# Sums of phi_k^T [v | 1] in blocks of three heads, or head by head in quarters of the array

## The chip, the cores and the metric

The kernel runs on one core of one Trainium2 chip. The metric is the device time of one execution in microseconds, as the median of several runs. Beside the runs there is one profiled execution, whose trace gives the start and length of each instruction on each engine: TensorE (PE, with its weight loads apart as PEld), VectorE (DVE), ScalarE (ACT), GpSimd (POOL), and the DMA queue that SyncE (SP) issues.

## The reference

Two layers, each an attention step and a dense step, on x of 2048 rows and 640 columns. The attention has 32 heads of 20 columns. Per head, q and k go through a small matrix w_phi and two softmaxes, so that phi has 40 columns:

```python
phi_k = concatenate([softmax(pk), softmax(-pk)], axis=-1)
kv  = einsum("bhsf,bhsd->bhfd", phi_k, v)      # per head: 40 x 20
z   = einsum("bhsf->bhf", phi_k)               # per head: 40
num = einsum("bhqf,bhfd->bhqd", phi_q, kv)
den = einsum("bhqf,bhf->bhq", phi_q, z)[..., None] + 1e-6
o = num / den                                  # then @ wo, and added to x
```

The dense step is x + mish(norm(x) @ w1 + b1) @ w2 with 1536 hidden columns. What matters here is kv and z: for each head, phi_k^T times [v | 1], a sum over all 2048 rows whose result is 40 x 21.

## The kernel before, in words

The rows are worked in 16 tiles of 128 (NT), two to a block (BT), eight blocks (NB). A layer has three parts. attend_first goes over the blocks and makes, for each tile, keys, values and queries: project multiplies the normalized rows with the weights (L344; weights and rows are split into a high and a low fp32r part, so each product is three matmuls), features makes the two softmaxes on ACT, DVE and POOL (L355 to L380), and the last of these steps, on POOL, is the multiplication with the reciprocal sums (L379). Queries are then turned and stored to DRAM (L425 to L429). attend_second reads them back (load, L521), multiplies them with the finished sums (average, L573), divides, and multiplies with wo. dense follows (L695 and L737).

The sum over rows that the change is about stands at the end of keys (L412 to L419). v is a row tile of 32 x 21 columns, each head's 20 values and a one; e is a row tile of 32 x 40 columns of phi_k. For each tile i the loop takes three heads at a time (11 groups g, the last of two heads): the stationary operand is v's 63 or 64 columns of the group, the moving operand is e's 120 columns. Even groups write output partitions 0 to 63, odd ones 64 to 127. What comes out is for three heads at once, 63 x 120, of which only the three blocks of 21 x 40 on the diagonal are wanted. The sums stay in two PSUM banks for the whole of attend_first: kva has pairs 0 to 3 of groups, kvz pairs 4 and 5. The operands are plain fp32.

finish_kv (L532) is the bridge between the two halves of the attention. It is a generator that attend_second advances: DVE copies the two banks to SBUF and multiplies them with a mask that keeps the diagonal blocks (L537); PE transposes the six pieces (L545); ACT and DVE bring them to kvb (L547 to L550), which has the group's 120 rows of phi on its partitions and, per group, 64 columns of head and value. In average, kvb is the moving operand, 63 columns at a time, against 64 rows of turned queries (L573).

The order of the instructions is set by a scheduler with a time model over the whole block (L816). In attend_second and in the first steps the order on PE and SP is that of the program (manual_schedule, L448 and L611). There, finish_kv's steps alternate with those of rest (L503), the projection of the last tile's queries, whose L344 products stand between the sum, the transposes and the first average.

PSUM has eight banks: mm_tile takes two at a time (two buffers, L66), one_tile one (four buffers, L69); kva and kvz are two of those four while the sum runs.

Of the kernel before, what the change touches and what calls it, by code (L numbers as in the profile page):

```python
# [29 lines left out]
HC = D // 2  # L30
EW = 2 * D
GW = 3 * (DH + 1)
GP = 6
VW = H * (DH + 1)
SKEW = 2
LAYERS = 2
# [6 lines left out]
def kernel(  # L43
# [45 lines left out]
    nc.vector.memset(neg_half, -0.5)  # L89
    two = const.tile([P, 1], F32, name="two")  # L90
    nc.vector.memset(two, 2.0)
    mask = const.tile([P, 120], F32, name="mask")

    kvb = const.tile([120, GP, P], F32, name="kvb")

    stats = const.tile([P, NB, 2, BT], F32, name="stats")

# [289 lines left out]
    def attend_first(layer, x_src, first):  # L387


        def fetch_normed(b):  # L390
            if layer:
                return load_turned(n2_d[b], [row_tile] * 3)
            xt = fetch(x_src, b)
            norm_scale(b, [norm_stats(t, xt) for t in range(BT)])
            return xt

        pending = []

        def advance():
            for g in pending[::-1]:  # L400
                try:
                    next(g)
                except StopIteration:
                    pending.remove(g)

        def keys(xts, i, v):
            e = big_tile()
            yield from features(project(xts, i % BT, kv_ws, 0), e, False)
            yield
            if i % BT == 0 and BT < i < NT - BT:  # L410
                yield
            for g in range(G):  # L412
                p, n = divmod(g, 2)
                w, m = (120, 64) if g < 10 else (80, 42)
                acc, c = (kva, 120 * p) if p < 4 else (kvz, 120 * (p - 4))
                nc.tensor.matmul(acc[64 * n:64 * n + m, c:c + w], v[:, GW * g:GW * g + m],  # L416
                                 e[:, 120 * g:120 * g + w],
                                 start=(i == 0 and p in (0, 4)), stop=(i == NT - 1),
                                 skip_group_check=True)  # L419

        def queries(xts, i, ps=None):
            e = query_tile(i)
            yield from features(project(xts, i % BT, q_ws, 0) if ps is None else ps, e, True)

            nc.vector.transpose(e, e)  # L425
            b, t = divmod(i, BT)
            dst = e_d[b].rearrange("(j f) (t q s) -> t q f j s", f=32, t=BT, s=32)
            for q in range(4):
                nc.sync.dma_start(dst[t, q], e[32 * q:32 * q + 32].rearrange("f (j s) -> f j s", s=32))  # L429
                if b == NB - 1:  # L430
                    yield

        def values(xts, i, v):
            vv = v.rearrange("p (h d) -> p h d", d=DH + 1)
            act(vv[:, :, DH], ident[:, :H], AF.Copy, scale=0.0, bias=1.0)
            if i < BT:
                pv = project(xts, i, kv_ws, D, [one_tile(), one_tile()])
                for c in range(2):
                    act(vv[:, c * H // 2:(c + 1) * H // 2, :DH],
                        pv[c][:, :HC].rearrange("p (h d) -> p h d", d=DH), AF.Copy)  # L440
            else:
                pv = project(xts, i % BT, kv_ws, D)
                act(vv[:, :, :DH].rearrange("p (c h) d -> p c h d", c=2),
                    both(pv).rearrange("p c (h d) -> p c h d", d=DH), AF.Copy)
            yield

        if first is None:
            with tc.manual_schedule(engines={mybir.EngineType.SP}):  # L448
                bd = big_tile()[:120, :720].rearrange("p (t c) -> p t c", t=6)
                nc.sync.dma_start(bd[:, :3], phi_bd[:, :3])  # L450
                raw = load_raw(0, range(3))
                xt = fetch_normed(0)
                nc.sync.dma_start(bd[:, 3:], phi_bd[:, 3:])
                raw += load_raw(0, range(3, 6))
                nxt = normed(0, xt).all()
                q_ws = [r2_pair(k) for k in range(KD)]
                fold_phi(q_ws, bd, raw)
                kv_ws = load_v_weights()
                raw = load_raw(1)
            nc.sync.dma_start(mask, head_mask)  # L460
        else:
            nxt, kv_ws = first
            q_ws = load_q_weights()
        for b in range(NB):
            xts = nxt
            order = ("k0", "k1", "v0", "v1", "q0", "q1")
            if b == 0:
                order = ("v0", "q0", "v1", "k0", "q1", "k1")
            elif b == 1:
                order = ("k0", "q0", "k1", "v0", "q1", "v1")  # L470
            elif b == NB - 1:
                order = ("k0", "k1", "v0", "v1", "q0")
            vs = [v_tile() for _ in range(BT)]
            for n, (kind, t) in enumerate(order):
                t = int(t)
                i = b * BT + t
                if b == 0 and n == 1:
                    if layer:
                        load_k_weights(kv_ws)
                if b == 0 and n == 3:  # L480
                    if layer == 0:
                        fold_phi(kv_ws, bd, raw)
                    kva, kvz = one_tile(), one_tile()
                if b == NB - 1 and n == 3:
                    loaded = {0: load(0)}
                if b + 1 < NB:
                    if n == 0:
                        xt = fetch_normed(b + 1)
                    elif n == 2:
                        nxt = xt if layer else normed(b + 1, xt)  # L490
                    elif n > 2:
                        nxt.step()
                g = {"k": lambda: keys(xts, i, vs[t]), "q": lambda: queries(xts, i),
                     "v": lambda: values(xts, i, vs[t])}[kind]()
                next(g)
                advance()
                pending.append(g)
            if b == 1:
                if layer == 0:
                    spill_qk_weights(kv_ws, q_ws)  # L500
                o_ws = load_o_weights()

        def rest():  # L503

            ps = [one_tile(), one_tile()]
            project_half(ps[0], xts, 1, q_ws, 0, 0)
            advance()
            advance()
            yield
            project_half(ps[1], xts, 1, q_ws, 0, 1, range(3))  # L510
            yield
            project_half(ps[1], xts, 1, q_ws, 0, 1, range(3, KD))
            pending.append(queries(xts, NT - 1, ps))
            next(pending[-1])
            while pending:
                yield
                advance()

        return kva, kvz, o_ws, loaded, rest()

    def load(b):  # L521

# [6 lines left out]
        nc.sync.dma_start(tc_[:80, 0], e_d[b][1200:])  # L529
        return [(ta, tb)[g // 5][:, (g % 5) * BLK:(g % 5 + 1) * BLK] for g in range(10)] + [tc_[:, 0]]  # L530

    def finish_kv(kva, kvz, mask):  # L532

        acc, acz = row_tile(), row_tile()
        for src, dst, p1, n, w in ((kva, acc, P, 4, 120), (kvz, acz, P, 1, 120), (kvz, acz, 42, 1, 80)):
            c = 120 if w == 80 else 0
            nc.vector.tensor_tensor(dst[:p1, c:c + n * w].rearrange("p (n w) -> p n w", n=n),  # L537
                                    src[:p1, c:c + n * w].rearrange("p (n w) -> p n w", n=n),
                                    mask[:p1, :w].unsqueeze(1).to_broadcast([p1, n, w]), op=ALU.mult)
        yield  # L540
        for src, q0, n in ((acc, 0, 4), (acz, 4, 2)):
            ps = one_tile().rearrange("p (n c) -> p n c", n=4)
            for q in range(n):
                p1, w = (P, 120) if q0 + q < 5 else (42, 80)
                nc.tensor.transpose(ps[:w, q, :p1], src[:p1, 120 * q:120 * q + w], ident[:p1, :p1])  # L545
            if n == 4:
                act(kvb[:, :4], ps[:120], AF.Copy)  # L547
            else:
                nc.vector.tensor_copy(kvb[:, 4], ps[:120, 0])
                nc.vector.tensor_copy(kvb[:80, 5, :42], ps[:80, 1, :42])  # L550
        yield

    def attend_second(x_src, x_dst, acc, fetches, makes, fetch_next, begin_next):
        kva, kvz, o_ws, loaded, rest = acc
        rows = {}
        div = [None]

# [5 lines left out]
        def average(b, t):  # L563
# [3 lines left out]
            for g in range(G):  # L567
# [3 lines left out]
                for q in range(2):  # L571
                    s0 = t * P + 64 * q
                    nc.tensor.matmul(  # L573
                        po[64 * q:64 * q + 64, c, GW * j:GW * j + w], phs[g][:n, s0:s0 + 64],
                        kvb[:n, g // 2, 64 * (g % 2):64 * (g % 2) + w], start=True, stop=True)
            o = row_tile()
            den = work.tile([P, H], F32, tag="r", name="den", bufs=2)
            pv = [po[:, c, :(DH + 1) * n].rearrange("p (h d) -> p h d", d=DH + 1)
# [30 lines left out]
                return mv  # L609

        with tc.manual_schedule(engines={mybir.EngineType.PE, mybir.EngineType.SP}):  # L611
            kv = finish_kv(kva, kvz, mask)
            next(rest)
            next(kv)
            loaded[1] = load(1)
# [283 lines left out]
```

## Time and profile before

| what | value |
|---|---|
| runs | 1396.43, 1398.02, 1398.83 us; median 1398.02 |
| the profiled execution's own time | 1396.09 us |
| its span, first to last instruction | 1394.3 us |
| mean granted TensorE clock | 0.999 |
| matmuls at L416 as the trace counts them | 704 multiplies, 704 weight loads |

The page gives the busy time of each engine and what it waited for. A group such as "L416 PE MATMUL one<-big,v" is line 416 of the kernel, its engine and operation, the tile it writes (one) and those that it reads (big is e, v is v), and the shape. The ends of matmuls are modelled in the trace, so how fast PE works is read from the starts of successive rows: a row of the timeline has its start, its length up to the end of the last of its instructions, and how many follow each other (x22).

### The profile page before, as it was taken

To read this page: it belongs to the slowest core of one execution; us is meant where nothing else is said; L and a number is where in the kernel's file an instruction comes from. 1 tells how busy PE (TensorE), PEld (TensorE's weight loads), DVE (VectorE), ACT (ScalarE), POOL (GpSimd) and SP (SyncE) were. 2 spreads that over 40 slices of the span, in tenths; PEclk is the share of its full clock that TensorE was granted. 3 is DMA by queue.
4 is the path that set the end of the run, shared out by engine and by line. 5 is a ranking of instruction groups with operands and counts; after the bars stand their busy time and mean duration, and the time that the engine had idled before them with its cause. 6 is when DMAs were issued, how large, how long until landed. Compare 5 with 4: busy or idle time off the path is not lost. (4 is left out here: it accounts for less than half of the span.)

```text
span 1394.3 us, 28137 instructions
## 1 busy us (share of the span) xinstructions
PE 1380.7 (99%) x11528; PEld 1367.0 (98%) x11528; DVE 1075.5 (77%) x1820; ACT 583.3 (42%) x973; POOL 440.0 (32%) x334
## 2 busy tenths in 40 slices
PE   7999999999999999999999999999999999999998
PEld 7999999999999999999999999999999999999998
DVE  5797877796698877788769988888767876777775
ACT  4444433321355454545454333332235444444443
POOL 1353443343422221222234434343342211211112
PEclk9999999999999999999999999999999999999999
DMA  8533333689633432343474333357976212333200
GB/s 328 162 79 54 67 52 58 184 228 307 235 86 95 114 84 62 83 114 95 122 261 87 71 57 58 65 107 231 288 257 200 76 25 72 95 95 95 75 22 20
DMA packets 350035, 169.57 MB, mean 122 GB/s; under 512 B 286866, under 2 KB 323458, under 8 KB 349906
## 3 DMA queue, kind: packets, MB, share of 16 engines
q1 hardware_dynamic: 349906, 167.78, 44.2%
q8 instruction: 90, 1.47, 0.4%
q14 instruction: 39, 0.32, 0.1%
HBM read 104.82 MB, written 62.91 MB: 120 GB/s over the span
## 5 line engine op out<-in xcount | busy, mean ns | idle before, releaser
L737 PE MATMUL mm<-r2h,ol 128*128 128x320 f32 x1280 | 304.7, 309 | 0.0
L721 POOL TENSOR_TENSOR ol<-big,ol 128x512 fp32r<-128x512 f32 (+1 forms) x98 | 129.8, 1324 | 483.5 <-ACT ol L720 407.3
L695 PE MATMUL one<-xtl,r1h 128*128 128x256 f32 x960 | 268.2, 279 | 0.0
L695 PE MATMUL one<-xth,r1l 128*128 128x256 f32 x960 | 268.0, 279 | 0.0
L695 PE MATMUL one<-xth,r1h 128*128 128x256 f32 x960 | 265.9, 279 | 0.0
L737 PEld LDWEIGHTS mm<-r2h,ol 128*128 128x128 f32 x1280 | 219.1, 188 | 0.0
L737 PE MATMUL mm<-r2l,ol 128*128 128x320 f32 x640 | 197.3, 309 | 0.0
L344 PE MATMUL mm<-r1h,xth 128*128 128x320 f32 x600 | 187.3, 312 | 0.0
L344 PE MATMUL mm<-r1h,xtl 128*128 128x320 f32 x600 | 186.0, 310 | 0.7 <-DVE xtl L286 0.7
L344 PE MATMUL mm<-r1l,xth 128*128 128x320 f32 x600 | 186.0, 310 | 0.0
L695 PEld LDWEIGHTS one<-xtl,r1h 128*128 128x128 f32 x960 | 180.4, 188 | 0.0
L695 PEld LDWEIGHTS one<-xth,r1l 128*128 128x128 f32 x960 | 180.4, 188 | 0.0
L695 PEld LDWEIGHTS one<-xth,r1h 128*128 128x128 f32 x960 | 179.6, 188 | 0.0
L710 DVE TENSOR_SCALAR big<-big 128x512 f32<-128x512 f32 (+1 forms) x98 | 57.1, 583 | 109.9 <-ACT big L708 109.7
L379 POOL TENSOR_TENSOR r<-r,r 128x1280 f32<-128x1280 f32 x32 | 75.8, 2368 | 163.1 <-DVE r L378 157.3
L737 PEld LDWEIGHTS mm<-r2l,ol 128*128 128x128 f32 x640 | 120.2, 188 | 0.0
L712 ACT ACTIVATE big<-big,two 128x512 f32<-128x512 f32 (+1 forms) x98 | 70.1, 715 | 116.2 <-DVE big L711 116.1
L708 ACT ACTIVATE big<-one,b1s 128x256 f32<-128x256 f32 x192 | 80.8, 467 | 90.1 <-PE one L695 89.6
L720 ACT ACTIVATE ol<-big 128x512 fp32r<-128x512 f32 (+1 forms) x98 | 61.0, 622 | 136.0 <-DVE big L719 135.9
L344 PEld LDWEIGHTS mm<-r1h,xth 128*128 128x128 f32 x600 | 112.8, 188 | 1.3
L344 PEld LDWEIGHTS mm<-r1h,xtl 128*128 128x128 f32 x600 | 112.7, 188 | 1.3 <-DVE xtl L286 1.0
L344 PEld LDWEIGHTS mm<-r1l,xth 128*128 128x128 f32 x600 | 112.8, 188 | 0.1
(129 smaller groups left out, 3156.1 us busy)
## 6 DMA issues: line engine op xcount, KB each, us to landing
e_d<-r SPq DMA_DIRECT2D x128, 160.0 KB, 4.0
big<-e_d SPq DMA_DIRECT2D x32, 640.0 KB, 6.6
x_d<-xt SPq DMA_DIRECT2D x23, 640.0 KB, 3.9
xt<-x_d SPq DMA_DIRECT2D x22, 640.0 KB, 4.3
n_d<-xn SPq DMA_DIRECT2D x176, 80.0 KB, 2.1
xt<-in_x SPq DMA_DIRECT2D x16, 640.0 KB, 5.9
xn<-x_d SPq DMA_DIRECT2D x28, 320.0 KB, 4.2
v<-n_d SPq DMA_DIRECT2D x30, 256.0 KB, 3.3
```

The lines of the kernel that those rows point to most:

```text
L344: nc.tensor.matmul(ps[:, :HC], a[:, sl], r, start=(k == 0 and n == 0), stop=(k == KD - 1 and n == 2))
L379: nc.gpsimd.tensor_tensor(eg, eg, r.unsqueeze(2).to_broadcast([P, 2 * H, DH]), op=ALU.mult)
L695: nc.tensor.matmul(ph[:, j, :], l, r, start=(n == 0), stop=(n == 3 * KD - 1))
L708: exps[0] = nc.scalar.activation(part(ta, 0)[:, j - js.start], ph[:, j, :], AF.Exp, bias=b1s[:, 2 * pr + j:2 * pr + j + 1]).ins
L710: nc.vector.tensor_scalar_min(e, e, E_CAP)
L712: nc.scalar.activation(r, n, AF.Ln, bias=two)
L720: nc.scalar.activation(ah[:, js], n, AF.Copy)
L721: nc.gpsimd.tensor_tensor(al[:, js], n, ah[:, js].bitcast(F32), op=ALU.subtract)
L737: nc.tensor.matmul(pys[t][:, c, :HC], l[:, j, sl], r, start=(f == 0 and n == 0), stop=(f == KF - 1 and n == 2))
```

## The change

The sum is made head by head. The 32 heads of a tile are 32 matmuls of 21 stationary and 40 moving columns. Four heads stand side by side in output partitions 0, 32, 64 and 96, nine such rows make 360 columns, so that one bank holds all sums: head h = 3 (4a + j) + i stands in quarter j and columns 40 (3a + i). The first quarter gets nine heads, the second nine, the third eight, the fourth six. Each matmul computes a wanted block and nothing else. Since 11 partitions of each quarter are never written, the bank is first set to zero. In finish_kv DVE copies 360 columns, PE transposes three pieces of 120, and three DVE operations spread each head's 21 columns to the three places of its group, multiplied with a mask of 120 x 3 that is one where the row belongs to that head. kvb gets the same content as before, one row of 64 columns per group. The average's operands have the same sizes.

```diff
-    mask = const.tile([P, 120], F32, name="mask")
-    kvb = const.tile([120, GP, P], F32, name="kvb")
+    mask = const.tile([120, 3], F32, name="mask")
+    kvb = const.tile([120, 12, 64], F32, name="kvb")
...
-            for g in range(G):
-                p, n = divmod(g, 2)
-                w, m = (120, 64) if g < 10 else (80, 42)
-                acc, c = (kva, 120 * p) if p < 4 else (kvz, 120 * (p - 4))
-                nc.tensor.matmul(acc[64 * n:64 * n + m, c:c + w], v[:, GW * g:GW * g + m],
-                                 e[:, 120 * g:120 * g + w],
-                                 start=(i == 0 and p in (0, 4)), stop=(i == NT - 1),
-                                 skip_group_check=True)
+            for r in range(9):
+                for j in range(4):
+                    h = 3 * (4 * (r // 3) + j) + r % 3
+                    if h < H:
+                        nc.tensor.matmul(kva[32 * j:32 * j + DH + 1, 40 * r:40 * r + 40],
+                                         v[:, (DH + 1) * h:(DH + 1) * (h + 1)], e[:, 40 * h:40 * h + 40],
+                                         start=(i == 0 and r == 0), stop=(i == NT - 1), skip_group_check=True)
...
-            nc.sync.dma_start(mask, head_mask)
+            nc.sync.dma_start(mask, bass.AP(tensor=head_mask.tensor, offset=head_mask.offset,
+                                            ap=[[1, 120], [120 * (DH + 1), 3]]))
...
-                    kva, kvz = one_tile(), one_tile()
+                    kva = one_tile()
+                    nc.vector.memset(kva[:, :360], 0.0)
...
-    def finish_kv(kva, kvz, mask):
-
-        acc, acz = row_tile(), row_tile()
-        for src, dst, p1, n, w in ((kva, acc, P, 4, 120), (kvz, acz, P, 1, 120), (kvz, acz, 42, 1, 80)):
-            c = 120 if w == 80 else 0
-            nc.vector.tensor_tensor(dst[:p1, c:c + n * w].rearrange("p (n w) -> p n w", n=n),
-                                    src[:p1, c:c + n * w].rearrange("p (n w) -> p n w", n=n),
-                                    mask[:p1, :w].unsqueeze(1).to_broadcast([p1, n, w]), op=ALU.mult)
+    def finish_kv(kva):
+
+        acc = row_tile()[:, :360]
+        nc.vector.tensor_copy(acc, kva[:, :360])
         yield
-        for src, q0, n in ((acc, 0, 4), (acz, 4, 2)):
-            ps = one_tile().rearrange("p (n c) -> p n c", n=4)
-            for q in range(n):
-                p1, w = (P, 120) if q0 + q < 5 else (42, 80)
-                nc.tensor.transpose(ps[:w, q, :p1], src[:p1, 120 * q:120 * q + w], ident[:p1, :p1])
-            if n == 4:
-                act(kvb[:, :4], ps[:120], AF.Copy)
-            else:
-                nc.vector.tensor_copy(kvb[:, 4], ps[:120, 0])
-                nc.vector.tensor_copy(kvb[:80, 5, :42], ps[:80, 1, :42])
+        ps = one_tile()[:120, :384].rearrange("p (a j m) -> p a j m", a=3, j=4)
+        for a in range(3):
+            nc.tensor.transpose(ps[:, a], acc[:, 120 * a:120 * a + 120], ident)
+        for a in range(3):
+            n = 4 if a < 2 else 3
+            nc.vector.tensor_tensor(
+                kvb[:, 4 * a:4 * a + n, :GW].rearrange("p j (i m) -> p j i m", i=3),
+                ps[:, a, :n, :DH + 1].unsqueeze(2).to_broadcast([120, n, 3, DH + 1]),
+                mask.unsqueeze(1).unsqueeze(3).to_broadcast([120, n, 3, DH + 1]), op=ALU.mult)
         yield
...
-                        kvb[:n, g // 2, 64 * (g % 2):64 * (g % 2) + w], start=True, stop=True)
+                        kvb[:n, g, :w], start=True, stop=True)
```

More of the change, by code (lines that the diff above doesn't have):

```diff
@@ L32 @@
 GW = 3 * (DH + 1)
-GP = 6
 VW = H * (DH + 1)
@@ L517, in rest @@
                 advance()
-        return kva, kvz, o_ws, loaded, rest()
+        return kva, o_ws, loaded, rest()
     def load(b):
@@ L530, in load @@
         return [(ta, tb)[g // 5][:, (g % 5) * BLK:(g % 5 + 1) * BLK] for g in range(10)] + [tc_[:, 0]]
-    def finish_kv(kva, kvz, mask):
-        acc, acz = row_tile(), row_tile()
-        for src, dst, p1, n, w in ((kva, acc, P, 4, 120), (kvz, acz, P, 1, 120), (kvz, acz, 42, 1, 80)):
-            c = 120 if w == 80 else 0
-            nc.vector.tensor_tensor(dst[:p1, c:c + n * w].rearrange("p (n w) -> p n w", n=n),
-                                    src[:p1, c:c + n * w].rearrange("p (n w) -> p n w", n=n),
-                                    mask[:p1, :w].unsqueeze(1).to_broadcast([p1, n, w]), op=ALU.mult)
-        yield
-        for src, q0, n in ((acc, 0, 4), (acz, 4, 2)):
-            ps = one_tile().rearrange("p (n c) -> p n c", n=4)
-            for q in range(n):
-                p1, w = (P, 120) if q0 + q < 5 else (42, 80)
-                nc.tensor.transpose(ps[:w, q, :p1], src[:p1, 120 * q:120 * q + w], ident[:p1, :p1])
-            if n == 4:
-                act(kvb[:, :4], ps[:120], AF.Copy)
-            else:
-                nc.vector.tensor_copy(kvb[:, 4], ps[:120, 0])
-                nc.vector.tensor_copy(kvb[:80, 5, :42], ps[:80, 1, :42])
+    def finish_kv(kva):
+        acc = row_tile()[:, :360]
+        nc.vector.tensor_copy(acc, kva[:, :360])
+        yield
+        ps = one_tile()[:120, :384].rearrange("p (a j m) -> p a j m", a=3, j=4)
[7 more added lines that the diff above has]
+                mask.unsqueeze(1).unsqueeze(3).to_broadcast([120, n, 3, DH + 1]), op=ALU.mult)
         yield
     def attend_second(x_src, x_dst, acc, fetches, makes, fetch_next, begin_next):
-        kva, kvz, o_ws, loaded, rest = acc
+        kva, o_ws, loaded, rest = acc
         rows = {}
@@ L611, in attend_second @@
         with tc.manual_schedule(engines={mybir.EngineType.PE, mybir.EngineType.SP}):
-            kv = finish_kv(kva, kvz, mask)
+            kv = finish_kv(kva)
             next(rest)
```

## The prediction

> **What bounds the kernel now.** I read the page first, then the stretches by stage, then PE's waits. The page: PE is the one engine without room.
>
> ```profile
> span 1394.3 us, 28137 instructions
> PE 1380.7 (99%) x11528; PEld 1367.0 (98%) x11528; DVE 1075.5 (77%) x1820; ACT 583.3 (42%) x973; POOL 440.0 (32%) x334
> ```
>
> The changed lines run in the first half of each attention layer (40 to 268 us and 710 to 945 us) and in the short bridge behind it. Busy time of each engine in those stretches:
>
> ```profile
> core 0: us, PE busy (x) PEld busy (x) DVE busy (x) ACT busy (x) POOL busy (x), PEclk, DMA share, GB/s
> 40.00:268.00 228.00, 228.00 (x1776) 224.47 (x1776) 183.51 (x243) 91.44 (x129) 104.33 (x64) 1.00 0.40 81
> 268.00:275.00 7.00, 6.57 (x129) 6.05 (x130) 3.92 (x15) 2.52 (x4) 0.00 (x0) 1.00 0.98 350
> 710.00:945.00 235.00, 233.92 (x1798) 230.74 (x1797) 197.39 (x223) 87.95 (x127) 102.80 (x55) 1.00 0.43 87
> ...
> PE mm L573 <- PE mm L573: 0.9, 2, 0.4
> PE mm L344 <- DVE xtl L286: 0.7, 1, 0.7
> PE one L416 <- POOL big L379: 0.3, 1, 0.3
> ```
>
> PE works through, DVE has about a fifth of its time free, and in these stretches PE waits for almost nothing (last three rows: us in total, times, longest). The granted clock is 1.00. So a microsecond that the sum at L416 takes less on PE is a microsecond off the span, and one that it takes more is one on top. The question is PE time alone.
>
> **What a block of the sum costs now.** A block is one tile of 128 rows: 11 matmuls at L416, 32 blocks in all.
>
> ```profile
> L416 PEld LDWEIGHTS one<-big,v x704: 118/137/137, 71.5 to 944.6; 128*64 128x64 f32 x160, 128*42 128x42 f32 x16
> L416 PE MATMUL one<-big,v x704: 232/266/318, 71.5 to 944.7; 128*64 128x120 f32 x160, 128*42 128x80 f32 x16
> ...
> 97.45 0.31 PE L344 MATMUL mm<-r1h,xtl 128*128 128x320 f32 x1
> 97.69 1.38 PE L416 MATMUL one<-big,v 128*64 128x120 f32 x22
> 98.99 0.41 PE L344 MATMUL mm<-r1h,xth 128*128 128x320 f32 x1
> ...
> 152.97 0.31 PE L344 MATMUL mm<-r1l,xth 128*128 128x320 f32 x1
> 153.20 2.54 PE L416 MATMUL one<-big,v 128*64 128x120 f32 x44
> 155.67 0.41 PE L344 MATMUL mm<-r1h,xtl 128*128 128x320 f32 x1
> ```
>
> 352 matmuls give 704 pairs of weight load and multiply: an fp32 matmul is two pairs. One block runs 1.38 us, two blocks in a row 2.54, so a block costs 2.54 - 1.38 = **1.16 us**; the rest of a burst, its start and end at the switch from and to L344, is paid once per burst and stays. 32 x 1.16 = 37 us of the span hang on this line.
>
> Are the two halves of 64 output partitions worked at the same time? Compare a whole-array fp32 product of the same 120 columns, and the narrower one of the averages:
>
> ```profile
> 17.81 1.38 PE L237 MATMUL one<-big,raw 120*128 120x120 f32 x10
> 271.25 1.38 PE L573 MATMUL mm<-kvb,big 120*64 120x63 f32 x40
> ```
>
> L237: ten in 1.38 us, about 0.12 us each. L416: 22 in 1.16 us, 0.053 each, for the same columns. So the halves do run side by side. The lower half has six of the eleven matmuls, five of 120 columns and one of 80, twice: 1360 columns in 1.16 us, 0.853 ns a column with what goes between. L573 gives the other bound: 40 in 1.38 us, (1.38 - 0.22) / 39 = 29.7 ns a pair, 59 ns in one half for 63 columns, 0.94 ns a column.
>
> **The change part by part.**
>
> (a) The sum. 32 matmuls of 40 columns a block, 64 pairs, in quarters. The first quarter has nine heads, 18 pairs. If four quarters run as independently as two halves do, one pair takes 40 x 0.853 = 34 ns to 40 x 0.94 = 37.5 ns in its quarter. The weight loads shrink too, from 64 columns to 21, so they do not become the longer part. 18 pairs: 0.61 to 0.68 us; I take 0.64, in the middle. A block saves 1.16 - 0.64 = 0.52 us, 32 blocks 16.6 us (15.4 to 17.6). The order of PE is unchanged around the bursts: the same 19 bursts, six of one block and 13 of two, with the same waits for POOL ahead of them.
>
> One burst gives 0.5 us back, since its second block waits for POOL and will wait longer:
>
> ```profile
> 767.11 1.38 PE L416 MATMUL one<-big,v 128*64 128x120 f32 x22
> 768.84 1.38 PE L416 MATMUL one<-big,v 128*64 128x120 f32 x22 [0.35 <-POOL big L379]
> ```
>
> (b) The bridge (finish_kv), twice. The first row is four alike whole transposes elsewhere: (0.60 - 0.27) / 3 = 0.11 us apart. Three of them take 0.49 against 0.87 for the six of now: 0.4 us saved, 0.8 in both layers.
>
> ```profile
> 138.52 0.60 PE L280 MATMUL one<-ident,xn 128*128 128x128 f32 x4
> 269.37 0.87 PE L545 MATMUL one<-ident,xn 128*120 128x128 f32 x6
> ...
> L537 DVE TENSOR_TENSOR xn<-one,mask x6: 223/276/659, 267.7 to 946.1; 128x480 f32<-128x480 f32 x2, 128x120 f32<-128x120 f32 x2, 42x80 f32<-42x80 f32 x2
> L116 ACT ACTIVATE kvb<-one x2: 579/580/581, 270.3 to 947.2; 120x512 f32<-120x512 f32 x2
> 268.29 0.81 DVE L371 TENSOR_TENSOR r<-m,r 128x640 f32<-128x640 f32 x1
> ```
>
> DVE now masks in three pieces of 659, 276 and 223 ns; it will copy 360 columns, about 0.5 us (360 / 480 of the 659). The nine products of L344 between sum and transposes hide this as they hide the masks, but the copy now stands behind L371 (0.81 us) in DVE's order and the sum ends 1 us sooner: I charge 0.2 us a layer (0 to 0.5). Behind the transposes ACT's 0.58 us and two DVE copies become three masked spreads of 252, 252 and 189 elements on DVE, some 0.35 us each by the same row. The six L344 products between hide the first; the first average needs the groups in that order, so the others run beside it. Cost nothing; without cover, at most 0.7 us a layer.
>
> (c) Behind the bridge PE comes 1.5 us sooner to averages whose operands arrive by DMA at a share of 0.98 (the stretch from 268 above). The loads wait for the sum too (their buffers are the keys' tiles) and so are issued sooner, but the engines are full. I charge 0.3 us a layer, bounds 0 and 1.5.
>
> (d) The memset of 128 x 360 runs on DVE early in each layer, long before the first sum; nothing waits. The mask's DMA has 360 pieces of one element in place of 128 rows:
>
> ```profile
> q1 hardware_dynamic: 349906, 167.78, 44.2%
> ```
>
> 0.442 x 16 x 1394 us / 349906 = 28 ns a packet; 232 more over 16 engines are 0.4 us, at a time when PE waits for loads. Charged in full (0 to 0.4). The bank that comes free takes no wait away: no row above is a wait for a PSUM tile of this kind. POOL's and SP's orders keep their instructions but for the mask.
>
> **Sum**: -16.6 + 0.5 - 0.8 + 0.4 + 0.6 + 0.4 = -15.5 us. The profiled execution took 1396.1 us (span 1394.3); the median of the runs shown, 1398.0, is 1.9 above it. 1396.1 - 15.5 = 1380.6, with 1.9 more **1382 us**. With the bounds of (a), (b) and (c), 1378 to 1387.
>
> **Rivals.**
>
> 1. *PE isn't handed pairs fast enough: slower.* The forecast needs a pair every 35.5 / 4 = 8.9 ns. The fastest pair that any row sustains is the 29.7 ns of L573. If that is the limit, a block is 64 x 29.7 = 1.90 us, 0.74 more than now, 23.7 us in all; with the other parts 1421 us. The point that decides is 1.16 us / 64 = 18.1 ns a pair: above it the change loses. Midway between, 24 ns, gives 32 x (1.54 - 1.16) = 12 us more, 1409 us. For it: the pairs grow from 704 to 2048 and none was ever seen closer than 29.7 ns over a stretch. Against it: L573's pairs are explained by the columns of one half (59 ns for 63 columns and 64 weights), so nothing shows the supply as the limit there. And after a long wait of PE, supply shows by itself:
>
> ```profile
> 951.30:951.36 0.06, 0.00 (x0) 0.01 (x1) 1.00 1.09 444
> 951.36:951.37 0.01, 0.00 (x0) 0.01 (x1) 1.00 0.34 103
> 951.37:951.38 0.01, 0.00 (x1) 0.01 (x1) 1.00 0.00 0
> 951.38:951.39 0.01, 0.01 (x2) 0.01 (x2) 1.00 3.28 1332
> ```
>
> These are L573's own instructions: (x) counts multiplies, then loads, in flight. The second load and multiply belong to the other half, and the rest of the first half's two pairs stands before them in the program. So four instructions came within 0.04 us of the first load, 18 ns a pair at worst, and within 20 ns of the first multiply, 10 ns a pair at worst. That is a burst of four, not a stream of 64; hence the chance I leave. The Trainium skill, TensorEngine Tiling (Array Packing), Instruction Overhead, speaks against this change: each matmul carries about 60 cycles, so no tiling factor should be taken from a dimension that is already small. By the 25 ns that TensorE: Matmul & The Clock Gate (Back-to-back issue gap) gives for this, an estimate is 64 x 25 = 1.6 us a block and some 14 us more for the sum, if the floor counts across quarters; no row here shows it across halves.
>
> 2. *Supply between the two.* From 8.9 to 18 ns a pair the gain shrinks in proportion: 1387 to 1395 us.
>
> 3. *No change: multiplies start in program order, so only neighbours overlap.* A matmul's two pairs use one quarter, so the second must wait for the first, and only it overlaps the next matmul's first. A block is then 32 x 34 to 37.5 ns = 1.09 to 1.20 us against 1.16: 1395 to 1401 us. Against it: in the rows just above, the other half's multiply is in flight within 20 ns of the first, before the first half's second one, which the first holds back for 59 ns. The Trainium skill, TensorE: Matmul & The Clock Gate, Part 3, states this order (matmuls start and end strictly in program order); the trace disagrees, with the 20 ns.
>
> **How the numbers follow.** Forecast 0.50; rival 2 0.13; rival 3 0.09, rival 1 0.28. A measurement of this kernel tells about 0.2% from no change, 2.8 us: faster is below 1395.2, slower above 1400.8. Faster 0.50 + 0.13 = 0.63, same 0.09, slower 0.28. The range starts at 1377, a little below the forecast's own 1378 (0.06 left out), and ends at 1411, which takes in rival 1 up to a little over its midway (0.13 left out).
>
> **What would show it.** Right: L416 with 2048 multiplies, a burst of one block about 0.9 us long and of two 1.5, four multiplies in flight in one stretch of 10 ns, nothing new in PE's waits. Rival 1: bursts above 1.4 and 2.6 us, gaps between the quarters' multiplies. Rival 3: bursts as long as now, two multiplies in flight. Wrong in the rest: waits of PE at L416 for POOL or at the averages for DMA that add up to more than 2 us, or a burst that costs more at its switches.

## The result, and the profile after

The changed kernel takes **1384.58 us** (median of four runs, 1383.90 to 1385.02) against 1397.87 us of the kernel before in the same comparison: ratio 0.9905, 95% interval 0.9888 to 0.9923, or 13.3 us less. Two later comparisons gave 15.4 us (1384.01 against 1399.36, ratio 0.9889, 0.9875 to 0.9903) and 13.7 us (1384.61 against 1398.26, ratio 0.9903, 0.9887 to 0.9920). The forecast was 1382 in a range of 1377 to 1411.

The profiled execution took 1385.02 us with a span of 1383.2, so by the two profiled executions it is 11.1 us. The page, with its span and busy time by engine:

```profile
span 1383.2 us, 30808 instructions
PE 1364.8 (99%) x12866; PEld 1351.4 (98%) x12866; DVE 1082.0 (78%) x1820; ACT 583.1 (42%) x971; POOL 440.5 (32%) x334
```

PE is still the engine without room, and it has more instructions in less time. L416 by groups (count, then minimum, median and maximum of one in ns):

```profile
L416 PEld LDWEIGHTS one<-big,v x2048: 96/103/108, 72.7 to 933.6; 128*21 128x21 f32 x187
L416 PE MATMUL one<-big,v x2048: 202/202/216, 72.8 to 933.7; 128*21 128x40 f32 x187
```

The length of one multiply (202 ns) is latency and tells nothing of the rate. That is read from the bursts. The timeline of PE in the changed kernel (start, length, how many), a burst of one block and one of two:

```profile
97.61 0.30 PE L344 MATMUL mm<-r1h,xtl 128*128 128x320 f32 x1
97.85 0.83 PE L416 MATMUL one<-big,v 128*21 128x40 f32 x64
98.61 0.41 PE L344 MATMUL mm<-r1h,xth 128*128 128x320 f32 x1
...
121.67 0.31 PE L344 MATMUL mm<-r1h,xtl 128*128 128x320 f32 x1
121.91 1.48 PE L416 MATMUL one<-big,v 128*21 128x40 f32 x128
123.31 0.42 PE L344 MATMUL mm<-r1h,xth 128*128 128x320 f32 x1
```

A block costs 1.48 - 0.83 = **0.65 us**, where it cost 1.16: 64 pairs, one every 10 ns on average. The ends of the bursts are as before: 0.24 us from the last L344 to the first L416, some 0.13 us from the last L416 to the next L344. The first hundredths of a microsecond of the first of these bursts, L416 alone ((x) counts multiplies, then weight loads, in flight):

```profile
97.84:97.85 0.01, 0.00 (x1) 0.00 (x1) 1.00 0.74 128
97.85:97.86 0.01, 0.01 (x2) 0.01 (x2) 1.00 1.10 154
97.86:97.87 0.01, 0.01 (x4) 0.01 (x5) 1.00 0.82 115
```

Four multiplies are in flight within 30 ns of the first. The stretches by stage and what PE waited for (us in total, times, longest):

```profile
40.00:268.00 228.00, 227.00 (x2588) 223.05 (x2589) 193.17 (x258) 93.97 (x133) 104.37 (x64) 1.00 0.42 92
710.00:945.00 235.00, 230.50 (x2642) 227.03 (x2641) 205.66 (x244) 89.14 (x130) 101.09 (x53) 1.00 0.44 95
```

```profile
PE one L416 <- POOL big L379: 2.8, 1, 2.8
PE mm L344 <- DVE xtl L286: 1.7, 2, 1.3
PE mm L569 <- PE mm L569: 0.9, 2, 0.4
PE mm L733 <- ACT ol L716: 0.8, 1, 0.8
PE one L344 <- DVE xt L599: 0.7, 2, 0.6
```

In the second layer's stretch PE is now busy for 230.5 of 235 us, where it was 233.9. That is where part of the gain went. (L569 is the average, L573 before; L733 and L716 were L737 and L720.) The two worst waits stand together, at the second layer's first blocks. PE, then DVE, then POOL in the changed kernel (in brackets: idle before, and who ended it):

```profile
761.14 0.83 PE L416 MATMUL one<-big,v 128*21 128x40 f32 x64
764.72 0.83 PE L416 MATMUL one<-big,v 128*21 128x40 f32 x64 [2.75 <-POOL big L379]
...
769.08 0.42 PE L344 MATMUL mm<-r1h,xtl 128*128 128x320 f32 x1 [1.28 <-DVE xtl L286]
```

```profile
756.59 0.81 DVE L371 TENSOR_TENSOR r<-m,r 128x640 f32<-128x640 f32 x1
...
757.78 0.62 DVE L286 TENSOR_TENSOR xtl<-xn,xth 128x512 fp32r<-128x512 f32 x1
758.33 2.99 DVE L369 TENSOR_TENSOR big<-big,m 128x640 f32<-128x640 f32 x1
761.24 0.54 DVE L378 RECIPROCAL r<-r 128x64 f32<-128x64 f32 x1
...
762.38 2.84 DVE L286 TENSOR_TENSOR xtl<-xn,xth 128x512 fp32r<-128x512 f32 x1
```

```profile
758.00 2.63 POOL L379 TENSOR_TENSOR big<-big,r 128x1280 f32<-128x1280 f32 x1 [5.83 <-DVE r L378]
761.92 2.75 POOL L379 TENSOR_TENSOR big<-big,r 128x1280 f32<-128x1280 f32 x1 [1.29 <-DVE r L378]
```

And the first of these products in the kernel before:

```profile
762.12 2.63 POOL L379 TENSOR_TENSOR big<-big,r 128x1280 f32<-128x1280 f32 x1 [5.83 <-DVE r L378]
```

The chain is to be read backwards. The second sum waits for POOL's L379 of 761.92, that one for DVE's reciprocal of 761.24, and DVE has no gap in front of it. It spends 2.99 us on L369, which starts at 758.33 while POOL's L379 of 758.00 runs. That product ends at 760.63, L369 at 761.32, 0.69 later; L371 on as many elements takes 0.81 where POOL is idle. The next pair is alike: POOL's second product ends at 764.67, DVE's L286, started in its course, at 765.22, 0.55 later, and L286 took 0.62 at 757.78. So each of these two DVE operations advances as if it had to wait for POOL's product first. The kernel before has the same two (2.98 and 2.84 us, beside POOL's products of 762.12 and 766.03), so the change did not make them. PE had to wait here for 0.35 us before the change. Its first sum now starts 5.97 us earlier by the span's start (761.14 against 767.11) and is 0.55 us shorter, so PE is ready for the second 6.52 us earlier, while POOL's products come only 4.1 us earlier (758.00 against 762.12). The difference, 2.4 us, is what the wait grew by.

The bridge in the changed kernel: PE's three transposes, the average after the wait that it had before, and DVE's copy and spreads by groups (after the first bar: us in total, mean ns of one; after the second: idle before them):

```profile
262.59 0.54 PE L540 MATMUL one<-ident,xn 128*120 128x128 f32 x3
...
267.15 1.38 PE L569 MATMUL mm<-kvb,big 120*64 120x63 f32 x40 [0.43 <-PE mm L569]
```

```profile
L543 DVE TENSOR_TENSOR kvb<-one,mask 120x252 f32<-120x252 f32 x4 | 1.5, 415 | 1.3 <-PE one L540 1.3
L536 DVE COPY xn<-one 128x360 f32<-128x360 f32 x2 | 1.1, 526 | 0.0
```

### The profile page after: what moved, and what is told of

It is laid out like the page before. It is cut to its first block, busy times and chain, and to the rows that moved or that the text cites. A ratio compares the mean times of both kernels' runs of the same rounds, so it can differ in the third digit from the quotient of the medians.

```text
span 1383.2 us, 30808 instructions
## 1 busy us (share of the span) xinstructions
PE 1364.8 (99%) x12866; PEld 1351.4 (98%) x12866; DVE 1082.0 (78%) x1820; ACT 583.1 (42%) x971; POOL 440.5 (32%) x334
## 5 line engine op out<-in xcount | busy, mean ns | idle before, releaser
L733 PE MATMUL mm<-r2h,ol 128*128 128x320 f32 x1280 | 305.1, 309 | 0.8 <-ACT ol L716 0.8
L733 PEld LDWEIGHTS mm<-r2h,ol 128*128 128x128 f32 x1280 | 219.1, 188 | 1.3 <-ACT ol L716 1.1
L733 PE MATMUL mm<-r2l,ol 128*128 128x320 f32 x640 | 197.3, 309 | 0.0
L344 PE MATMUL mm<-r1h,xtl 128*128 128x320 f32 x600 | 185.8, 310 | 1.7 <-DVE xtl L286 1.7
L344 PE MATMUL mm<-r1h,xth 128*128 128x320 f32 x600 | 187.4, 312 | 0.0
L344 PE MATMUL mm<-r1l,xth 128*128 128x320 f32 x600 | 186.0, 310 | 0.0
L379 POOL TENSOR_TENSOR r<-r,r 128x1280 f32<-128x1280 f32 x32 | 75.8, 2370 | 149.4 <-DVE r L378 143.5
L733 PEld LDWEIGHTS mm<-r2l,ol 128*128 128x128 f32 x640 | 120.2, 188 | 0.0
L716 ACT ACTIVATE ol<-big 128x512 fp32r<-128x512 f32 (+1 forms) x98 | 61.0, 622 | 136.3 <-DVE big L715 136.2
L344 PEld LDWEIGHTS mm<-r1h,xtl 128*128 128x128 f32 x600 | 112.7, 188 | 2.2 <-DVE xtl L286 2.1
L344 PEld LDWEIGHTS mm<-r1h,xth 128*128 128x128 f32 x600 | 112.7, 188 | 0.7
L344 PEld LDWEIGHTS mm<-r1l,xth 128*128 128x128 f32 x600 | 112.7, 188 | 0.1
```

The source lines that it names most:

```text
L344: nc.tensor.matmul(ps[:, :HC], a[:, sl], r, start=(k == 0 and n == 0), stop=(k == KD - 1 and n == 2))
L379: nc.gpsimd.tensor_tensor(eg, eg, r.unsqueeze(2).to_broadcast([P, 2 * H, DH]), op=ALU.mult)
L716: nc.scalar.activation(ah[:, js], n, AF.Copy)
L733: nc.tensor.matmul(pys[t][:, c, :HC], l[:, j, sl], r, start=(f == 0 and n == 0), stop=(f == KF - 1 and n == 2))
```

## The experiments

The theory, Q: each quarter works off its own pairs one after another, 35.5 ns each, and the four quarters run at once, so a block costs 18 rounds. The rival, S: the instruction stream or the small shape sets the block's time, whatever quarter a pair goes to. The first four kernels, e1 to e4, have one run each, beside 1398.23 us of the kernel before.

**e1, all heads in one quarter.**

```diff
-nc.tensor.matmul(kva[32 * j:32 * j + DH + 1, 40 * r:40 * r + 40],
+nc.tensor.matmul(kva[0:DH + 1, 40 * r:40 * r + 40],
...
-start=(i == 0 and r == 0),
+start=(i == 0 and r == 0 and j == 0),
```

> The changed kernel with all 32 heads' sums written to the first quarter (four heads land on the same 360 columns, so the sums are not the reference's); the number of pairs, their sizes and their order are the same. Theory Q (a pair holds its quarter for 36 ns, four quarters work side by side, and the supply of pairs is not the limit): a block of 64 pairs takes 64 x 36 = 2.3 us in place of 0.65, so 32 blocks cost 53 us more, about 1437 us. Rival S (the 0.65 us of a block are the supply of pairs, 10 ns each, whichever quarter): no change, 1384 to 1386 us.

1432.67 us. PE's timeline, the burst of one block and one of two:

```profile
103.46 2.47 PE L416 MATMUL one<-big,v 128*21 128x40 f32 x64
...
129.16 4.77 PE L416 MATMUL one<-big,v 128*21 128x40 f32 x128
```

A block is 4.77 - 2.47 = 2.30 us, 64 pairs at 36 ns, one after another. The shapes and the number of pairs are the same; only the place is another: Q holds and S falls. The time is 4 us below the 1437 expected. The trace has none of the waits at L416, L344 and L733 that the changed kernel has (6.0 us in its profiled execution), and 1.6 us more of waits at L237, at the start, so the difference is in the waits and not in the block.

**e2, two places, output partitions 0 and 64.**

```diff
-nc.tensor.matmul(kva[32 * j:32 * j + DH + 1, 40 * r:40 * r + 40],
+nc.tensor.matmul(kva[64 * (j % 2):64 * (j % 2) + DH + 1, 40 * r:40 * r + 40],
...
-start=(i == 0 and r == 0),
+start=(i == 0 and r == 0 and j < 2),
```

> The same, with the heads written to the first and the third quarter alone (two heads land on the same columns, so the sums are not the reference's). Theory Q: the first of the two has 17 heads, 34 pairs of 36 ns, so a block takes 1.22 us, 0.57 more, 18 us in 32 blocks: about 1403 us, slightly above the kernel before, which has two halves and three times the products. Rival S: no change, 1384 to 1386 us.

1401.03 us. The same two bursts:

```profile
99.95 1.40 PE L416 MATMUL one<-big,v 128*21 128x40 f32 x64
...
124.57 2.62 PE L416 MATMUL one<-big,v 128*21 128x40 f32 x128
```

2.62 - 1.40 = 1.22 us a block, a little over the 1.16 of before, and the 1.22 expected. With two at a time the sum by heads brings nothing, although it computes a third of the products. The whole gain is that four run at a time.

**e3, quarter after quarter.** The same pairs in another order.

```diff
-            for r in range(9):
-                for j in range(4):
+            for j in range(4):
+                for r in range(9):
```

> The changed kernel with the two loops of the sum exchanged: all heads of the first quarter, then all of the second, and so on; every product and its place are the same. Theory Q with a short look ahead (PE finds work for an idle quarter only a few instructions behind): the quarters work one after the other, a block takes nearly 64 x 36 = 2.3 us, about 1437 us. Theory Q with a long look ahead (a whole block): little change, up to 1390 us. Rival S: no change, 1384 to 1386 us.

1417.81 us, between the two values expected.

```profile
101.63 2.10 PE L416 MATMUL one<-big,v 128*21 128x40 f32 x64
...
126.96 3.89 PE L416 MATMUL one<-big,v 128*21 128x40 f32 x128
```

3.89 - 2.10 = 1.79 us a block, against 2.30 with no overlap and 0.65 with the loops as the change has them. The next quarter's first pair starts when some 15 of the 18 pairs before it have started: the 16th start of the burst at 101.63 comes 6 ns behind the 15th, while the starts before it, all in one quarter, are 35 to 44 ns apart. So PE passes a blocked pair, but only by about three pairs. With the quarters in this order the kernel is slower than the one before the change (1417.81 against 1398.23): the order of the loops is as much a part of the change as the quarters.

**e4, eight columns in place of 40; e5, four weights besides.** These look for the supply. Of the matmul, the three operands alone are shown; both are edits of the changed kernel, and the rest of the sums is left out.

```diff
-kva[32 * j:32 * j + DH + 1, 40 * r:40 * r + 40], v[:, (DH + 1) * h:(DH + 1) * (h + 1)], e[:, 40 * h:40 * h + 40]
+kva[32 * j:32 * j + DH + 1, 40 * r:40 * r + 8],  v[:, (DH + 1) * h:(DH + 1) * (h + 1)], e[:, 40 * h:40 * h + 8]    # e4
+kva[32 * j:32 * j + 4, 40 * r:40 * r + 8],       v[:, (DH + 1) * h:(DH + 1) * h + 4],   e[:, 40 * h:40 * h + 8]    # e5
```

> The changed kernel with 8 of each head's 40 moving columns (the other 32 columns of the sums are left out); the same 64 pairs a block in the same order. Theory Q: a pair now holds its quarter for its weights, 21 columns, or for a floor of its own, some 20 to 27 ns, so a block takes 0.36 to 0.49 us in place of 0.65, 5 to 9 us off in 32 blocks: about 1376 to 1380 us. Rival S: the supply of 10 ns a pair stays, a block stays at 0.65 us and the time at 1384 to 1386 us.

> The changed kernel with 8 of each head's 40 moving columns and 4 of its 21 stationary ones (the rest of the sums is left out); the same 64 pairs a block. The kernel with 8 columns alone took 0.56 us a block, 8.8 ns a pair. If that was the weight load of 21 columns in a quarter, a block now takes 0.3 to 0.45 us. If it is the supply of instructions, it stays at 0.55 to 0.57 us: then the changed kernel, whose full rounds need a pair every 8.9 ns, runs right at the limit of the supply.

1379.71 us for e4; 1381.60 for e5, one run beside 1398.26. The bursts of each, e4 first:

```profile
99.08 0.69 PE L416 MATMUL one<-big,v 128*21 128x8 f32 x64
...
122.27 1.25 PE L416 MATMUL one<-big,v 128*21 128x8 f32 x128
```

```profile
99.64 0.66 PE L416 MATMUL one<-big,v 128*4 128x8 f32 x64
...
122.51 1.22 PE L416 MATMUL one<-big,v 128*4 128x8 f32 x128
```

Both step by **0.56 us a block**, 8.8 ns a pair, though e4 streams a fifth of the columns and e5 loads a fifth of e4's weights. For e4 neither expectation came true: Q had 0.36 to 0.49 us a block and S 0.65, and only the time, 1379.71, lies in Q's range. In both the first thirty or so pairs of a burst start 6.4 to 6.9 ns apart and the rest slower, as if the first ones had been fetched ahead. The first ones also show that 8.8 ns is not what a pair holds its quarter for: four times 6.4 is 26 ns, four times 8.8 is 35. So the columns set 0.65 and the supply 0.56: the changed kernel runs just above the supply. A version with still smaller products can gain no more than the 0.09 us a block between them.

The kernels from here on have four or five runs each.

**f0, the changed kernel again**, for the comparison in one place.

> The changed kernel itself, beside the next three on the same chip: 1383.5 to 1385.5 us.

1384.01 us (1382.31 to 1386.56), beside 1399.36.

**f1, the second bank held**: a second tile stays taken for the sum and eight of its columns are cleared and copied.

```diff
-                    kva = one_tile()
+                    kva, kvz = one_tile(), one_tile()
+                    nc.vector.memset(kvz[:, :8], 0.0)
...
+        nc.vector.tensor_copy(acc[:, 600:608], kvz[:, :8])
```

> The changed kernel with a second PSUM tile held through the sum, as the kernel before had it (a memset of 8 columns and a copy of them stand in for its use). If the freed bank gives nothing, as the prediction has it: within 1 us of the changed kernel. If the freed bank is part of the gain: 2 us or more slower.

1383.75 us (1382.95 to 1384.26), ratio 0.9885 (0.9872 to 0.9899) to the kernel before. Its runs lie within those of f0: the bank that comes free gives nothing that these runs can tell.

**f2, the averages in quarters**: the change's idea at another place.

```diff
-                for q in range(2):
-                    s0 = t * P + 64 * q
+                for q in range(4):
+                    s0 = t * P + 32 * q
...
-po[64 * q:64 * q + 64, c, GW * j:GW * j + w], phs[g][:n, s0:s0 + 64]
+po[32 * q:32 * q + 32, c, GW * j:GW * j + w], phs[g][:n, s0:s0 + 32]
```

> The changed kernel with the averages also in quarters: 32 rows of turned queries at a time in place of 64, 88 pairs in place of 44 for a row tile. Theory W (a half's pair of the averages is held to 58.5 ns by its 64 weights, though its 63 columns need 54): with 32 weights the columns alone hold it, 22 pairs x 54 ns = 1.19 us in place of 1.29, 32 times, 3 us faster: about 1381.5 us. Rival: 58.5 ns is what 63 columns take, or the supply of 88 pairs costs something: no gain, 1384 us or more.

1404.56 us (1403.20 to 1405.79), ratio 1.0035 (1.0021 to 1.0048): 20.5 us slower than the changed kernel. In its timeline the rounds of four themselves are quick: 65 multiplies in 1.09 us, (1.09 - 0.22) / 64 = 13.6 ns a pair, 54 ns a round, where a half took 59 ns with its 64 weights. But then PE stands still:

```profile
267.50 1.09 PE L569 MATMUL mm<-kvb,big 120*32 120x63 f32 x65 [0.56 <-PE mm L569]
272.48 0.54 PE L569 MATMUL mm<-kvb,big 120*32 120x63 f32 x12 [3.89 <-issue]
```

"issue" means that the engine waited for nothing that the profile shows. All of f2's waits of this kind, and the stretch around the longest (PE, PEld, DVE, ACT, POOL, then the granted clock and the DMA share):

```profile
PE mm L569 <- issue: 13.9, 8, 3.9
...
PE one L344 <- issue: 1.0, 2, 0.8
```

```profile
268.00:272.50 4.50, 0.61 (x48) 0.45 (x36) 0.87 (x2) 0.00 (x0) 0.00 (x0) 0.78 1.06 360
272.50:277.30 4.80, 4.80 (x101) 4.37 (x105) 3.21 (x8) 1.47 (x3) 0.00 (x0) 0.50 0.53 149
```

PE idles for 14.9 us in ten gaps, and after the idle 4 us its granted clock is 0.50 for the next 4.8 us of work. The clock is halved in the same way behind two more of the gaps. The DMA queues of f2 from 268 to 274.6 us (packets, MB, share of 16 engines):

```profile
q1 hardware_dynamic: 2041, 2.23, 105.5%
q8 instruction: 2, 0.03, 2.1%
```

The instructions come by DMA themselves, in packets of 16 KB (q8; 0.03 MB in two), and here they share engines that are full. Twice the instructions in the same time ran dry. The packets' times bear it out: the longest gap starts at 268.59 us, a packet of q8 starts at 269.88 and lands at 270.97, and PE goes on at 272.48. All nine gaps of more than 0.3 us end so, 1.3 to 1.5 us after a packet of q8 has landed. That the packets come late because the engines are full is argued; no run took the loads away. The Trainium skill, Runtime: NRT & Kernel Launch (Instruction fetch mechanics), gives blocks of 16 KB with 256 instructions each and holds the fetch to be hidden behind the issue of instructions. The traces agree with the size: q8 brings 90 packets in the kernel before and 100 in the changed one, and 256 times that is 23040 and 25600, where PE has 23056 and 25732 multiplies and weight loads. They do not agree that it is always hidden, by f2's gaps.

**f3, the second layer's first sums one step later**, so that the wait for POOL goes.

```diff
-            if i % BT == 0 and BT < i < NT - BT:
+            if i % BT == 0 and (0 if layer else BT + 1) <= i < NT - BT:
```

> The changed kernel with the second block's sum of the second layer put one step later in the program, so that 16 products of L344 (16 x 0.147 = 2.4 us) stand between it and the first. Theory: the wait of 2.8 us for POOL in the middle of that burst is part of what the change gave back, so most of it goes, and one more switch costs 0.3 us: about 2 us faster, 1382.5 us. Rival: VectorE has no idle time in that stretch, so PE only waits later, at the next stage's rows: within 0.7 us of the changed kernel.

1386.53 us (1386.13 to 1387.45), ratio 0.9906 (0.9893 to 0.9920): 2.5 us above f0, not below it. The waits of PE in f3 (its list has none for POOL at L416):

```profile
PE mm L344 <- DVE xtl L286: 4.0, 3, 2.4
...
PE mm L344 <- ACT r L116: 0.5, 1, 0.5
```

The 1.3 us of f0's wait for POOL are gone and the waits for DVE grow from 1.7 to 4.0. The rival was right in kind, since DVE is the bound in this stretch and the wait changes its place; its size, within 0.7 us of the changed kernel, was not. A part of the 2.5 us is the clock, as g0 shows below.

The last three stand beside 1398.26 us. **g0** is the changed kernel once more. **g1** gives DVE less there: in the second layer the subtraction L369 of the first block's keys goes to POOL, as the queries' does already. **g2** does it for two blocks.

```diff
-            yield from features(project(xts, i % BT, kv_ws, 0), e, False)
+            yield from features(project(xts, i % BT, kv_ws, 0), e, bool(layer) and i < BT)
```

> The changed kernel itself, beside the next two on the same chip: 1383 to 1385.5 us.

> The changed kernel with the first subtraction of the keys of the second layer's first block (L369) on POOL in place of VectorE, as the queries have it. Theory: VectorE has no idle time in that stretch, and the two operations take 0.8 to 3.0 us of it, most where POOL's multiplication runs beside them, so PE's waits there (1.3 to 2.8 us at the sum and 1.3 us behind it) shrink: 1 to 3 us faster, about 1382 us. Rival: POOL, which hands over the block's last step, becomes the one that is late, and the wait at the sum stays or grows: 1384 us or more.

> The same for the first two blocks of the second layer. Theory: nothing more to gain, since PE does not wait in the second block: as the kernel with one block, within 1 us. Rival: POOL's sequence of longer operations is late in the second block: slower than with one block by 1 us or more.

g0 1384.61 us (1384.20 to 1385.26); **g1 1381.94** (1381.45 to 1382.48), ratio 0.9884 (0.9869 to 0.9899); g2 1381.69 (1380.01 to 1385.10), ratio 0.9885 (0.9870 to 0.9901). g1's runs all lie below g0's: 2.7 us less. The second block adds nothing that these runs can tell. PE's waits in g1:

```profile
PE mm L344 <- DVE xtl L286: 1.4, 2, 1.0
PE one L344 <- DVE xt L599: 1.0, 1, 1.0
```

No wait for POOL is left at L416, though POOL has more to do. The chain was bound by DVE, and POOL's product had waited for it.

Not all of the 2.7 us are the waits themselves. g0's trace shows a cost that the lists of waits don't have, behind its wait for POOL (PE's row, then the stretch behind it with PE, PEld, DVE, ACT, POOL, the granted clock, the DMA share):

```profile
763.62 0.92 PE L416 MATMUL one<-big,v 128*21 128x40 f32 x64 [2.34 <-POOL big L379]
```

```profile
764.20:767.60 3.40, 3.40 (x35) 3.29 (x23) 3.40 (x4) 0.00 (x0) 1.23 (x1) 0.50 0.15 41
```

For 3.4 us the granted clock is 0.50. The products of L344 start 0.27 us apart there and 0.15 behind it, so about 1.5 us are lost, an estimate from these two spacings. f3 has the same 3.4 us at 0.50 behind its wait of 2.4 us, from 768.2 us, and so have e4 and e5, with waits of 2.8 and 3.1 us for POOL there. The profiled execution of the first comparison has a wait of 2.8 us there and no halved clock behind it, and f0 and g1 have none either. So a wait of this size can cost more than itself, but not each time, and no run here shows what decides it.

## Why the prediction was right, step by step

**The sum (a)** was right in size. 0.65 us a block against 0.64; added up between successive starts at L416, 37.4 us before became 23.3, of which 2.4 are the longer wait for POOL, so the sum itself gave 16.6, as forecast. e1 and e2 show the reason to be the one given: quarters work independently, a pair costs its quarter 36 ns. That the supply allowed it was luck in part: a full round needs a pair every 8.9 ns, e4 and e5 measured 8.8, and nothing that the prediction had showed a stream so fast.

**The wait for POOL** was the right place and too small. Forecast were 0.5 us more. The changed kernel's executions show 1.3 to 2.8 in all (0.35 before). The step took it that only the first sum's own 0.5 us would be missing; but PE arrives 6 us sooner after the earlier bursts and the chain through DVE and POOL came only 4.1 sooner. The mark set for "wrong in the rest", more than 2 us of such waits, was passed in the profiled execution (2.8) and in g0 (2.3), and not in f0 (1.3). f3 and g1 show that DVE sets it.

**Waits that the sum had at nothing**: "nothing new in PE's waits" failed. By the lists of waits, L344 for DVE's xtl grew from 0.7 to 1.7 us, and 0.8 at L733 and 0.7 at L344 for xt are new, 2.5 us. In f0 it is 1.2, so the size changes from one execution to the next. The halved clock of g0, some 1.5 us, is a term that the sum did not have at all. The step treated a microsecond off PE as a microsecond off the span; with the other engines' chains so near behind, only part is.

**The bridge (b)**: the transposes gave 0.74 us by the starts (0.8 forecast) and 0.26 more at the switch behind them. The charge of 0.4 for the copy behind L371 was not due: no wait of PE stands there, and the average's list holds only the wait that it had.

**The averages (c)**, charged 0.6, cost nothing in the profiled execution and in f0: 0.43 us twice, as in the kernel before, and released by PE itself, not by DMA. In g0 PE waits there for 1.1 us more, of the kind "issue" and ending 1.4 us after a packet of q8, as in f2, and f1 has 0.7 of this kind: where the averages cost something, it was by this sign the instructions that came late, not the operands.

**The mask (d)** was charged 0.4 at the start. There something is late that stays open. The first L416 starts at 72.75 us in the changed kernel, at 71.48 before; all traces of kernels with the change have it between 72.75 and 74.6. Of these 1.27 us, 0.86 are there when PE first multiplies for the keys (L344 at 43.46 us against 42.60), so most of it arises in the preparation of the weights. The mask's transfer itself lands no later (6.5 us after its issue against 6.8). There is one trace of before only, so whether the change does this or that execution was early can't be told. From the first L416 to the end the gain is 12.4 us in the profiled execution (11.1 + 1.27) and 15.7 in f0 (span 1380.3, first L416 at 73.21; before, span 1394.3 and 71.48).

Put together for the profiled execution: the forecast -15.5, less the charges that were not due (0.4 copy, 0.6 averages, 0.4 mask) and 0.2 more from the transposes, is -17.1; 1.9 more wait for POOL, 2.5 of the other waits and 1.3 at the start make -11.4, where the spans differ by 11.1. By the medians 13.3, 15.4 and 13.7 us came off, so the term that was mis-sized is the waits given back, between 1.7 us (f0: 0.45 and 1.2) and 4.4 us (the profiled execution) more than the 0.5 charged. That the forecast came within 2.6 us of the median is luck to some degree: the charges that were not due, 1.4 us in all, made up for a part of these waits.

Some ends in the prediction, 1378, 1409 and 1421, are counted from the profiled execution's 1396.1 without the 1.9 us that the forecast adds. From 1398.0 the same parts give about 1380, 1411 and 1422; nothing here hangs on it.

**Rival 1** falls: pairs are supplied every 8.8 ns, against the 8.9 that the forecast needed. The point at which the change loses, 18.1 ns, is far off, but rival 2 was near: from some 9 to 10 ns on the supply would have set the block. The Trainium skill's rule, TensorEngine Tiling (Array Packing), Instruction Overhead, that a matmul of one column has the same latency as one of 60, would have made a block 1.6 us by the estimate in the prediction, if it counted across quarters; e4's 8.8 ns and the 10 ns here show that it doesn't. **Rival 2** falls with it. **Rival 3**, starts in program order, falls by the 0.65 us and by e3, where the next quarter's first pair starts ahead of three that stand before it in the program. The Trainium skill, TensorE: Matmul & The Clock Gate, Part 3, states that matmuls start and end strictly in program order; e3's trace disagrees across quarters, by these three pairs. The rival isn't without grounds: the order is passed by about three pairs and not more.

## What to carry to other kernels

Small matmuls gain from standing side by side in quarters only if successive instructions go to different quarters, and if a round of four costs more than the 35 ns in which four pairs are supplied. Count the instructions too: the same idea lost 20 us where twice as many ran beside full DMA engines. When an engine is at 99%, look at what each burst waits for, and ask by how much that chain moves forward; the microseconds saved in front of it come off only as far as it does. Look at the granted clock behind each wait of a few microseconds as well: it can take as much again.

## What the runs showed of the hardware that was not expected

- A pair of weight load and multiply of 8 columns is supplied every 8.8 ns in a long burst, with 4 weights as with 21; the first thirty or so of a burst come 6.4 to 6.9 ns apart (e4, e5).
- A blocked pair is passed by about three pairs and not more (e3: 1.79 us a block).
- Instructions ran out for up to 3.9 us at a DMA share of 1.06, PE went on 1.3 to 1.5 us after their packet had landed, and the granted clock was 0.50 for the 4.8 us of work behind the longest gap (f2).
- Behind waits of 2.3 to 3.1 us (g0, f3, e4, e5) the granted clock fell to 0.50 for 3.4 us; behind one of 2.8 us in the profiled execution of the changed kernel it did not.
- A DVE operation on two SBUF tensors that starts while POOL's product L379 runs ends a fixed time after that product, whatever was left of it. In the changed kernel's trace this holds for all 14 of L369 and L371 (0.68 to 0.70 us after it) and for all six of L286 with 512 columns of xn (0.55): L369 took 2.99 us where it takes 0.81 alone, L286 2.84 where another, started just before POOL's product, took 0.62. Where L286 reads its rows from a PSUM tile (one) it takes 0.67 to 0.69 us beside POOL's product, and four of six end before it. DVE's sums (L377), on one tensor, take some 1.4 to 1.5 us throughout.
